# Window attention with one 64-column score tile a head, and value matmuls in quarters

## The chip, the cores and the metric

The kernel runs on one core of a Trainium2 chip. TensorE (PE) multiplies matrices out of SBUF into PSUM, VectorE (DVE) and ScalarE (ACT) work elementwise on SBUF and PSUM, GpSimd (POOL) on SBUF, and SyncE (SP) issues most transfers. The engines run side by side and wait for one another by semaphores; each executes its own instructions in the order in which they were written. The metric is the device time of one execution in microseconds.

## The reference

Two stages, one behind the other, all in fp32.

Attention with a sliding window: batch 8, heads 8, sequence 576, head width 64. A token attends to itself and the 63 tokens before it in its sequence.

```python
scores = scale * np.matmul(q, k.transpose(0, 1, 3, 2))
rel = pos[:, None] - pos[None, :]
mask = (rel >= 0) & (rel < window)          # window = 64
scores = np.where(mask, scores, -1000000000.0)
scores = scores - np.max(scores, axis=-1, keepdims=True)
attn = np.exp(scores)
attn = attn / (np.sum(attn, axis=-1, keepdims=True) + 1e-09)
return np.matmul(attn, v).astype(np.float32)
```

Then a mixture of experts on the 4608 rows of 512 columns: logits `x @ w_gate` plus a bias by modality, the best of 8 experts for each row, its softmax weight as a gate, and `gate * (relu(x @ w1[e]) @ w2[e])` with 1024 hidden columns.

## The kernel before, in words

The sequence is cut into blocks of 64 tokens, nine to a batch entry. Two neighbouring blocks make a pair, so that there are 36 pairs. A token of a block can attend to tokens of its own block that are not later than it, and to tokens of the block before that are less than 64 back. In its own block that is the lower triangle with the diagonal; in the block before it is the strict upper triangle. The first block of a batch entry has no block before it: those are blocks 0, 9, 18 and so on, and pairs 0, 4, 9, 13, 18, 22, 27 and 31 hold one.

The program is one loop over steps `s` (line 1023), written out by hand: no scheduler reorders it, and each engine's queue is the order of the text. Step `s` works on several pairs at once: scores of pair `s`, transposes of the probabilities of pair `s-1`, values and scaled rows of pair `s-2`, router logits of pair `s-3`, and routing (`route1` to `route3`) and scattering of rows to an expert-sorted scratch in DRAM behind that. Also in each step, q and k of a later group of four blocks are transposed (`heads_t`, `heads_out`), v of pair `s` is loaded (`load_v`), and from step 5 on pieces of two experts' weights are loaded and split in two parts (`weights`).

From step `FIRST = 12` on, expert work is put between the attention's pieces: `gap` takes the next piece of a generator (`slot_pieces`), four pieces a step. A piece is 12 matmuls of 256 columns (`first`, line 304) or 6 of 512 columns (`second`, line 326), each for a slot of 256 rows. After step 39 the rest of the expert work runs alone to the end.

What the change touches in a step:

- `scores` (line 596): for each of four pairs of heads, four matmuls in quarters of the array. The row half (64 partitions of q and k) is the head's parity `a`, the column half is the block `c` of the pair. Each multiplies 64 queries with 128 keys: a block's own 64 and the 64 of the block before. Parity `a` goes to PSUM bank `sp[a]`.
- `minima` (line 617): on VectorE, for each of eight heads, one instruction adds a mask of three variants, scales by -1/8, writes to SBUF and gives the row's minimum.
- `exps` (line 633): on ScalarE, eight exponentials with the row's minimum as bias; each also gives the row's sum. They are issued in three portions over the step.
- `probs_t` (line 642), called twice: four 128x128 transposes on TensorE into one bank (`turn`, line 470), and a copy to SBUF on ScalarE (line 647).
- `values` (line 660): 16 matmuls, one for each head and block, of 128 keys by 64 queries by 64 columns. The 128 keys of the pair's second block are the pair's own rows of v (`vo`); those of the first block need the block before, so that a second tile `ve` holds the upper half of the pair before (`swap_upper`, VectorE) and the lower half of this pair (`swap_v`, GpSimd). The result is a bank of its own, `ps_a`.
- `values_out` (line 673): VectorE scales the rows by the reciprocal of the sums into `xa`; `x_t` transposes these rows, `logits` multiplies them with the gate's weights.

PSUM has eight banks: two `tp`, two scores, one values, three `ps_m` (`em`, `y0`, `y1`) which before step 12 also serve transposes (`turn_bank`, line 514).

## Time and profile before

| | us |
|---|---|
| median of three runs | 622.34 (620.07 to 623.06) |
| the profiled execution | 621.29 |
| its span, first to last instruction | 619.6 |
| scores of step 1 begin | 14.54 |
| scores of step 11 begin | 68.15 |
| scores of the last pair begin | 318.22 |

The granted TensorE clock is 0.992 over the span. In the profile, an instruction's line is that of the program above; a row of the line of time has start, duration, engine, line, operation and tiles, and `x4` means four instructions merged. A fp32 matmul leaves two records, an fp32r matmul or a transpose one. TensorE's ends are modelled, its starts are not.

### The profile page before, as it was taken

The page shows a single profiled execution, that of the slowest core. Times are in us where ns is not written, and L with a number is a line of the kernel's source. Part 1 is how long each engine was busy: PE and PEld are TensorE (multiplying, and loading weights), DVE is VectorE, ACT ScalarE, POOL GpSimd, SP SyncE. Part 2 cuts the span into 40 slices and gives each one's busy share as a digit, 9 for nine tenths or more (in the row PEclk, how much of TensorE's full clock was granted, in tenths as well). Part 3 has the DMA queues.
Part 4 walks back from the last instruction along what each step waited for, and adds up shares of the span by engine and source line. Part 5 has one row for each costly group of instructions (what it writes and reads, how often), then busy time and mean ns, then how long its engine had stood idle before and what let it go on. Part 6 is the DMA issues. An engine that isn't in the chain of part 4 may idle for free. (4 is left out here: it accounts for less than half of the span.)

```text
span 619.6 us, 17314 instructions
## 1 busy us (share of the span) xinstructions
PE 603.5 (97%) x6365; PEld 542.2 (88%) x6365; DVE 381.8 (62%) x1486; ACT 297.4 (48%) x933; POOL 139.7 (23%) x315
## 2 busy tenths in 40 slices
PE   8999889999999999999999999999999999999996
PEld 5888778889898998989898899999999989999986
DVE  3899987877776877667656465323324734776622
ACT  3999886765757555636463111111112513554411
POOL 6333422042313320321223131011001101102202
PEclk7999999999999999999999999999999999999999
DMA  9999865764675754463313034522243534678300
GB/s 163 216 234 246 204 183 166 188 188 126 167 205 123 194 135 99 137 155 84 107 54 103 35 103 167 174 69 69 51 155 116 167 126 137 203 239 249 108 18 21
DMA packets 158983, 88.08 MB, mean 142 GB/s; under 512 B 122618, under 2 KB 141616, under 8 KB 158768
## 3 DMA queue, kind: packets, MB, share of 16 engines
q1 hardware_dynamic: 150272, 67.45, 43.1%
q0 software_dynamic: 5888, 18.93, 8.1%
q8 instruction: 51, 0.84, 0.6%
q10 hardware_dynamic: 2736, 0.58, 0.5%
q14 instruction: 36, 0.29, 0.2%
HBM read 67.49 MB, written 23.91 MB: 148 GB/s over the span
## 5 line engine op out<-in xcount | busy, mean ns | idle before, releaser
L326 PE MATMUL y<-Whi,hh 128*128 128x512 f32 x288 | 116.9, 406 | 0.0
L638 ACT ACTIVATE ss<-ss,mn 128x128 f32<-128x128 f32 x288 | 112.6, 398 | 4.0 <-DMA wg<-in_moe_w_gate_dram 3.3
L326 PE MATMUL y<-Wlo,hh 128*128 128x512 f32 x288 | 112.7, 391 | 0.0
L326 PE MATMUL y<-Whi,hl 128*128 128x512 f32 x288 | 112.5, 391 | 0.0
L337 POOL DMA_INDIRECT out_dram<-y,id x36 | 39.8, 1107 | 232.7 <-DVE y L334 159.9
L313 DVE SCALAR_TENSOR_TENSOR hl<-em,hh 128x512 fp32r<-128x512 f32 x50 | 34.5, 690 | 92.8 <-ACT hh L312 82.1
L304 PE MATMUL em<-xh,Whi 128*128 128x256 f32 x400 | 83.7, 290 | 0.0
L312 ACT ACTIVATE hh<-em 128x512 fp32r<-128x512 f32 x50 | 29.6, 592 | 105.2 <-PE em L304 86.9
L304 PE MATMUL em<-xl,Whi 128*128 128x256 f32 x400 | 79.3, 280 | 0.0
L304 PE MATMUL em<-xh,Wlo 128*128 128x256 f32 x400 | 79.1, 279 | 0.0
L647 ACT COPY pT<-tp 128x512 f32<-128x512 f32 x57 | 31.4, 589 | 70.2 <-PE tp L470 60.9
L626 DVE CUSTOM_DVE_ANT_0 ss<-sp,masks 128x128 f32<-128x128 f32 x288 | 63.5, 286 | 2.4 <-PE sp L612 2.3
L326 PEld LDWEIGHTS y<-Whi,hl 128*128 128x128 f32 x288 | 54.1, 188 | 12.2
L304 PEld LDWEIGHTS em<-xh,Whi 128*128 128x128 f32 x400 | 62.3, 189 | 1.8
L326 PEld LDWEIGHTS y<-Whi,hh 128*128 128x128 f32 x288 | 54.2, 188 | 8.2
L326 PEld LDWEIGHTS y<-Wlo,hh 128*128 128x128 f32 x288 | 54.2, 188 | 7.9
L304 PEld LDWEIGHTS em<-xl,Whi 128*128 128x128 f32 x400 | 60.9, 188 | 0.0
L304 PEld LDWEIGHTS em<-xh,Wlo 128*128 128x128 f32 x400 | 60.9, 188 | 0.0
L638 ACT ACTIVATION_READ_ACCUMULATOR ss<-ss,mn 128x1 f32 x288 | 56.0, 195 | 0.0
L773 POOL DMA_INDIRECT xs_scratch<-xa,idx x36 | 36.4, 1012 | 81.8 <-DVE lm L716 40.3
L312 ACT ACTIVATE hh<-sp 128x512 fp32r<-128x512 f32 x22 | 13.2, 598 | 75.9 <-PE sp L304 73.9
L668 PEld LDWEIGHTS av<-ve,pT 128*64 128x64 f32 x576 | 36.3, 138 | 13.2 <-issue 8.2
(240 smaller groups left out, 1211.3 us busy)
## 6 DMA issues: line engine op xcount, KB each, us to landing
xt<-xs_scratch SPq DMA_DIRECT2D x72, 128.0 KB
vo<-in_v_dram SPq DMA_DIRECT2D x32, 256.0 KB
y<-in_moe_w_dram SPq DMA_DIRECT2D x32, 256.0 KB
vo<-in_moe_w_dram SPq DMA_DIRECT2D x24, 256.0 KB
ss<-in_moe_w_dram SPq DMA_DIRECT2D x24, 256.0 KB
xs_scratch<-xs_scratch SPq DMA_DIRECT2D x8, 514.0 KB
pT<-in_moe_w_dram SPq DMA_DIRECT2D x16, 256.0 KB
qk<-in_k_dram SPq DMA_DIRECT2D x14, 256.0 KB
```

The lines of the kernel that those rows point to most:

```text
L304: nc.tensor.matmul(out=hb[:, i * TP:(i + 1) * TP], lhsT=w[buf][:, c0:c0 + P], rhs=x[:, c * TP:(c + 1) * TP], start=(n == 0), stop=(n == le ...
L312: nc.scalar.activation(out=hh, in_=hb, func=AF.Relu),
L313: nc.vector.scalar_tensor_tensor(out=hl, in0=hb, scalar=0.0, in1=hh.bitcast(F32), op0=ALU.max, op1=ALU.subtract)))
L326: nc.tensor.matmul(out=sl["y", t], lhsT=h[:, i * TP + t * P:i * TP + (t + 1) * P], rhs=w[buf][:, c0:c0 + DM], start=(k == 0 and n == 0), s ...
L337: ins = nc.gpsimd.indirect_dma_start(out=out, out_offset=bass.IndirectOffsetOnAxis(ap=sl["id"][:, t:t + 1], axis=0), in_=y, in_offset=None ...
L626: nc.vector.tensor_tensor_reduce(out=ss[a][:, hp, :], in0=sp[a][:, hp * P:(hp + 1) * P], in1=mask, scale=-1.0 / 8.0, scalar=3.0e38, op0=AL ...
L638: nc.scalar.activation(out=ss[a][:, hp, :], in_=ss[a][:, hp, :], func=AF.Exp, bias=mn[:, h:h + 1], scale=-1.0, accum_out=sm[:, h:h + 1])
L647: nc.scalar.copy(out=pT, in_=pp)
L668: nc.tensor.matmul(out=by_block(av)[c * W64:(c + 1) * W64, a, :, hp, :], lhsT=pT[:, i:i + W64], rhs=(vo if c else ve)[p][:, 2 * hp + a, :] ...
L773: ins = nc.gpsimd.indirect_dma_start(out=xs, out_offset=bass.IndirectOffsetOnAxis(ap=idx[:, j:j + 1], axis=0), in_=xg[j], in_offset=None)
```

## The change

Each score row needs 64 probabilities, not 128: where the own key `j` is allowed (not later than the query), key `j` of the block before is not, and the other way round. So both triangles fit in one 64-column tile a head.

- `scores` makes the same 16 matmuls, but writes the own columns and the other columns to two halves of each bank, over one two-bank tile `sp`.
- `minima` copies, by predicate, the other half's scores into the own half above the diagonal (`above`); at a batch edge it fills that block's rows with a large negative number instead, in two half-height copies. Then one maximum over 64 columns and one subtraction, which writes the heads side by side to SBUF.
- `exps` is one exponential of 128x512; the sums are a VectorE reduction (`exp_sums`).
- `probs_t` makes four transposes and one copy for all eight heads. GpSimd then makes two tiles: the part of the block before (`left_of`) and, in place, the part of the own block (`from_`).
- `values` makes, for each of four pairs of heads, four matmuls with the own part and four with the other part that add to them, all of 64 keys by 64 queries by 64 columns, in quarters of the array. A first block of a batch entry has no other part. The result goes into the other half of the score banks of the current step, which that step's `minima` has read.
- V is loaded as 64 keys of two head parities, in four transfers a pair, into four buffers instead of three; `ve` and both swaps are gone.
- `ps_a` is gone and `tp` has three banks; `ss` has two buffers and `pT` four, and the weights that are loaded late use `vo` and `pT`.
- Order: values come after the pair's minima, the transposes of probabilities and the exponential; logits and row transposes come later in the step; all copies of transposed heads go to ScalarE.

```diff
-        sp = [ps_s.tile([P, 512], F32, name=f"sp{a}") for a in range(2)]
+        sp = st[p, "sp"] = ps_s.tile([P, 2, 512], F32, name="sp")
...
-                    out=sp[a][c * W64:(c + 1) * W64, hp * P:(hp + 1) * P], lhsT=qT[rows, place(g + c, hp), :],
+                    out=halves_of(sp[c * W64:(c + 1) * W64, a])[:, :, hp, :], lhsT=qT[rows, place(g + c, hp), :],
...
+        for rows, data in lots:
+            n = rows.stop - rows.start
+            nc.vector.copy_predicated(
+                out=own[rows], mask=above[rows].bitcast(I32)[:, None, None, :].broadcast_to([n, 2, HP, W64]),
+                data=data[rows])
+        mx = small.tile([P, 2, HP], F32, name="mn")
+        nc.vector.reduce_max(out=mx, in_=own, axis=AX.X)
+        ss = work.tile([P, HP, P], F32, name="ss", bufs=2)
+        nc.vector.tensor_tensor(
+            out=heads_of(ss), in0=own, in1=mx[:, :, :, None].broadcast_to([P, 2, HP, W64]), op=ALU.subtract)
...
+    def exps(p):
+        ss = st[p, "s"]
+        nc.scalar.activation(out=ss, in_=ss, func=AF.Exp, scale=1.0 / 8.0)
...
+        for t, m in ((other, left_of), (own, from_)):
+            nc.gpsimd.tensor_tensor(
+                out=t.rearrange("p (x i) -> p x i", i=W64), in0=own.rearrange("p (x i) -> p x i", i=W64),
+                in1=m[:, None, :].broadcast_to([P, 2 * HP, W64]), op=ALU.mult)
...
+    def values(p, sp):
+
+        own, other = st.pop((p, "p"))
+        for hp in range(HP):
+            for o in range(2):
+                for r, c in ((0, 0), (1, 1), (0, 1), (1, 0)):
+                    g = 2 * p + c
+                    edge = g % BPB == 0
+                    if o and edge:
+                        continue
+                    rows = slice(r * W64, (r + 1) * W64)
+                    i = hp * P + c * W64
+                    g -= o
+                    nc.tensor.matmul(
+                        out=sp[c * W64:(c + 1) * W64, r, 256:512].rearrange(
+                            "p (a c d) -> p a c d", a=2, d=R32)[:, :, hp, :],
+                        lhsT=(other if o else own)[rows, i:i + W64],
+                        rhs=vo[g // 2][rows, g % 2, hp, :].rearrange("p (a d) -> p a d", a=2),
+                        start=(o == 0), stop=(o == 1 or edge))
...
         if s < NPR:
             scores(s)
+            sp = st[s, "sp"]
...
             minima(s)
...
+        if s < FIRST:
+            part(0)
         if s == FIRST:
             run_later()
         if n_gap > 0 and s != FIRST:
             gap(it, True)
+        if 1 <= s <= NPR:
+            sums(s - 1)
+            probs_t(s - 1, turn_bank(s))
+        if s < NPR:
+            exps(s)
         if 2 <= s < NPR + 2:
-            x_t(s - 2, turn_bank(s) if s != FIRST else ps_m.tile([P, 512], F32, name="y0"))
+            if sp is None:
+                sp = ps_s.tile([P, 2, 512], F32, name="sp")
+            values(s - 2, sp)
+            values_out(s - 2)
+        if s < NPR:
+            exp_sums(s)
         run_later()
         tick(2)
...
+        if s < FIRST:
+            part(1)
+            choice()
+        else:
+            part(0)
+            choice()
...
+        rows_t()
+        if s >= FIRST:
+            part(1)
```

More of the change, by code (lines that the diff above doesn't have):

```diff
@@ L617, in minima @@
     def minima(p):
-        sp = st.pop((p, "sp"))
-        mask = masks[:, 1 if 2 * p % BPB == 0 else 2 if (2 * p + 1) % BPB == 0 else 0]
-        ss = [work.tile([P, HP, P], F32, name="ss", bufs=3) for _ in range(2)]
-        mn = small.tile([P, H], F32, name="mn")
-        for u in range(H):
-            a, hp = divmod(u, HP)
-            h = 2 * hp + a
-            nc.vector.tensor_tensor_reduce(
-                out=ss[a][:, hp, :], in0=sp[a][:, hp * P:(hp + 1) * P], in1=mask,
-                scale=-1.0 / 8.0, scalar=3.0e38, op0=ALU.add, op1=ALU.min,
-                accum_out=mn[:, h:h + 1])
@@ L630, in minima @@
-        sm = small.tile([P, H], F32, name="sm")
-        st[p, "s"] = ss, mn, sm
-    def exps(p, us):
-        ss, mn, sm = st[p, "s"]
-        for u in us:
-            a, hp = divmod(u, HP)
-            h = 2 * hp + a
-            nc.scalar.activation(
-                out=ss[a][:, hp, :], in_=ss[a][:, hp, :], func=AF.Exp,
-                bias=mn[:, h:h + 1], scale=-1.0, accum_out=sm[:, h:h + 1])
-    def probs_t(p, a, pp):
-        ss = st[p, "s"][0][a]
+        sp = st[p, "sp"]
+        own, other = (sp[:, :, x * 256:(x + 1) * 256].rearrange("p a (h j) -> p a h j", j=W64) for x in range(2))
@@ new lines, in minima @@
+        edge = [c for c in range(2) if (2 * p + c) % BPB == 0]
+        lots = [(slice(0, P), other)]
+        if edge:
+            fills = negs[:, None, None, :].broadcast_to([P, 2, HP, W64])
+            lots = [(slice(c * W64, (c + 1) * W64), fills if c in edge else other) for c in range(2)]
+        for rows, data in lots:
[3 more added lines that the diff above has]
+                data=data[rows])
@@ L644, in probs_t @@
+    def probs_t(p, pp):
+        ss = st.pop((p, "s"))
         for hp in range(HP):
             turn(pp[:, hp * P:(hp + 1) * P], ss[:, hp, :])
-        pT = work.tile([P, HP * P], F32, name="pT", bufs=2)
-        nc.scalar.copy(out=pT, in_=pp)
-        st[p, "p", a] = pT
+        own = work.tile([P, HP * P], F32, name="pT", bufs=4)
+        nc.scalar.copy(out=own, in_=pp)
+        other = work.tile([P, HP * P], F32, name="pT", bufs=4)
+        for t, m in ((other, left_of), (own, from_)):
+            nc.gpsimd.tensor_tensor(
+                out=t.rearrange("p (x i) -> p x i", i=W64), in0=own.rearrange("p (x i) -> p x i", i=W64),
+                in1=m[:, None, :].broadcast_to([P, 2 * HP, W64]), op=ALU.mult)
+        st[p, "p"] = own, other
@@ L911, in tile_window_attn_moe @@
     nc.gpsimd.memset(by_group(kT)[:, 1, :, GBLK - 1, :], 0.0)
[L914 to L933 removed]
+    above, left_of, from_ = (const.tile([P, W64], F32, name=nm) for nm in ("above", "left_of", "from"))
+    for t, step, op in ((above, 1, ALU.is_gt), (left_of, -1, ALU.is_gt), (from_, 1, ALU.is_ge)):
+        nc.gpsimd.memset(t, 1.0)
+        for h in range(2):
+            rows = slice(h * W64, (h + 1) * W64)
+            nc.gpsimd.affine_select(
+                out=t[rows], in_=t[rows], compare_op=op, fill=0.0, base=0,
+                pattern=[[step, W64]], channel_multiplier=-step)
+    negs = const.tile([P, W64], F32, name="negs")
+    nc.gpsimd.memset(negs, NEG)
     nc.gpsimd.memset(first_oh, 0.0)
@@ L1031, in tile_window_attn_moe, with part, rows_t, choice @@
         R = (s - 5) // GB if s >= 5 and j == 1 else -1
-        if 1 <= s < FIRST:
-            swap_upper(s - 1)
-        if 2 <= s < NPR + 2:
-            values(s - 2)
-            if s <= FIRST:
-                values_out(s - 2)
-        if 3 <= s < NPR + 3:
-            logits(s - 3, turn_bank(s) if s != FIRST else ps_m.tile([P, 512], F32, name="y0"))
-            if (s - 3) % GB == GB - 1:
-                route1((s - 3) // GB)
-        if FIRST < s < NPR + 2:
-            values_out(s - 2)
+        def part(i):
+            if not heads:
+                return
+            tp = turn_bank(s)
+            heads_t(G, *heads[i], tp)
+            heads_out(tp, G, *heads[i], nc.scalar.copy)
+        def rows_t():
+            if 2 <= s < NPR + 2:
+                x_t(s - 2, turn_bank(s))
+        def choice():
+            if 3 <= s < NPR + 3:
+                logits(s - 3, turn_bank(s))
+                if (s - 3) % GB == GB - 1:
+                    route1((s - 3) // GB)
+        sp = None
         if s < NPR:
             scores(s)
+            sp = st[s, "sp"]
             if s == FIRST:
```

137 lines of the change are left out of this document (39 added, 98 removed).

## The prediction

> **What bounds the kernel now.** I read the page's first part, then the stretches of the span, then TensorE's line of time.
>
> ```profile
> PE 603.5 (97%) x6365; PEld 542.2 (88%) x6365; DVE 381.8 (62%) x1486; ACT 297.4 (48%) x933; POOL 139.7 (23%) x315
> ...
> core 0: us, PE busy (x) PEld busy (x) DVE busy (x) ACT busy (x) POOL busy (x), PEclk, DMA share, GB/s
> 14.54:68.15 53.61, 50.50 (x992) 45.28 (x991) 49.80 (x281) 50.78 (x204) 19.78 (x38) 0.99 0.99 231
> 345.00:600.00 255.00, 255.00 (x1656) 232.20 (x1656) 124.20 (x257) 73.62 (x134) 35.47 (x76) 1.00 0.43 132
> ```
>
> There are two regimes. Before the expert work begins (step 12) TensorE, VectorE, ScalarE and the DMA engines are all over 90% busy together: no one of them is the bound, and a step is a tightly packed loop. The stretch 14.54 to 68.15 is ten steps, from the scores of step 1 to those of step 11: 5.36 us a step, with 4.98 us of VectorE, 5.08 of ScalarE and 1.98 of GpSimd in each. From step 12 on TensorE alone is full; after the attention (345 to 600) it is busy all of 255 us on work that the diff leaves alone. So whatever the attention's end moves by, the kernel's end moves by, and I sum that.
>
> ```profile
> 68.15 1.10 PE L612 MATMUL sp<-kT,qT 64*64 64x128 f32 x32
> ...
> 253.74 0.39 PE L326 MATMUL y<-Wlo,hh 128*128 128x512 f32 x1
> 253.96 0.40 PE L326 MATMUL y<-Whi,hl 128*128 128x512 f32 x1
> 254.28 0.27 PE L668 MATMUL av<-ve,pT 128*64 128x64 f32 x1
> 254.29 0.27 PE L668 MATMUL av<-vo,pT 128*64 128x64 f32 x1
> ...
> 255.22 0.22 PE L668 MATMUL av<-vo,pT 128*64 128x64 f32 x1
> 255.27 0.59 PE L697 MATMUL tp<-wg,xaT 128*64 128x8 f32 x16
> 255.79 1.10 PE L612 MATMUL sp<-kT,qT 64*64 64x128 f32 x32
> 256.82 1.09 PE L470 MATMUL tp<-ident_r,ss 128*128 128x128 f32 x8
> 257.67 0.48 PE L304 MATMUL em<-xh,Whi 128*128 128x256 f32 x2
> 258.00 0.40 PE L304 MATMUL em<-xh,Wlo 128*128 128x256 f32 x2
> 258.23 0.40 PE L304 MATMUL em<-xl,Whi 128*128 128x256 f32 x2
> ...
> 259.18 0.60 PE L470 MATMUL tp<-ident_r,xa 128*128 128x128 f32 x4
> 259.53 0.48 PE L304 MATMUL em<-xh,Whi 128*128 128x256 f32 x2
> ...
> 266.45 1.10 PE L612 MATMUL sp<-kT,qT 64*64 64x128 f32 x32
> ```
>
> This is one steady step, 255.79 to 266.45 (10.66 us). Starts matter, since ends are modelled: values hold TensorE 0.99 us (254.28 to 255.27), logits 0.52, scores 1.03, eight transposes 0.85, a piece of expert work 1.51 (257.67 to 259.18), four transposes 0.35.
>
> **The change, part by part, in a steady step.**
>
> *Transposes.* Eight become four: 0.85 - 0.35 = 0.50 us less on TensorE, which sets the end.
>
> *Values.* 32 records (16 matmuls, two records each) of 128 rows become 64 records of 64 rows, 48 in a pair with a batch edge. Scores already run in the same four quarters, with the same row half to one bank: their 32 records start within 1.10 - 0.27 = 0.83 us, 27 ns apart. The old values need 0.99 us for 16 turns of two records. If four quarters run at once, 64 records are again 16 turns: 0.99 us, no change. If instead each record costs the 27 ns of a score, 64 take 1.7 us, 0.75 more. I take 0: a score moves 128 columns, a value 64, so the score's row is no floor for it; 0.75 is kept for the range.
>
> *More changes of array shape.* Values, logits and scores now stand in one run; after the change each stands alone between pieces of 128-row work.
>
> ```profile
> 342.66 0.39 PE L326 MATMUL y<-Wlo,hh 128*128 128x512 f32 x1
> 342.89 0.39 PE L326 MATMUL y<-Whi,hl 128*128 128x512 f32 x1
> 343.21 0.64 PE L697 MATMUL tp<-wg,xaT 128*64 128x8 f32 x16
> 343.78 0.51 PE L304 MATMUL em<-xh,Whi 128*128 128x256 f32 x2
> 344.12 0.40 PE L304 MATMUL em<-xh,Wlo 128*128 128x256 f32 x2
> ```
>
> Logits alone, late in the kernel: the expert matmul ahead holds 0.32 us instead of 0.23 (342.66 to 342.89), and the first behind it 0.34 instead of the 0.23 of 258.00 to 258.23. So a border costs about 0.1. There are three borders now (into values, logits to scores, scores to transposes) and six afterwards: +0.30 us. The bounds are 0.15 and 0.45.
>
> *The wait of values.* This decides. Values are written into the "other" half of the two score banks, while VectorE still works through the "own" half of the same banks: predicated copy, maximum, subtraction. Does the matmul wait for the first only, or for all three? The start of the trace shows how two engines share a bank: VectorE and ScalarE each copy their own half of the columns.
>
> ```profile
> 7.90 0.42 DVE L593 COPY kT<-tp 128x256 f32<-128x256 f32 x1 [6.68 <-PE tp L470]
> 8.24 0.42 DVE L593 COPY qT<-tp 128x256 f32<-128x256 f32 x1
> ...
> 8.36 0.39 ACT L593 COPY kT<-tp 128x256 f32<-128x256 f32 x1 [3.26 <-DVE kT L593]
> 8.69 0.39 ACT L593 COPY qT<-tp 128x256 f32<-128x256 f32 x1
> ```
>
> ScalarE starts 0.04 us after VectorE's copy ends, twice, though the columns are disjoint: the order is kept by bank. I take it to hold for a matmul's write as well, so values wait for the subtraction. By the Trainium skill, PSUM — Partial Sum Buffer, "PSUM bank collisions raise a hardware error", PSUM is to be guarded by bank and partition quadrant and not by address; these rows agree, no run here shows a matmul's write yet, and without that rule the sum would be the rival "by columns" below.
>
> ```profile
> L626 DVE CUSTOM_DVE_ANT_0 ss<-sp,masks 128x128 f32<-128x128 f32 x288 | 63.5, 286 | 2.4 <-PE sp L612 2.3
> L679 DVE TENSOR_TENSOR xa<-av,rw 128x512 f32<-128x512 f32 x36 | 24.9, 691 | 2.6 <-PE av L668 0.5 <-DMA xs_scratch<-xa,idx 0.3
> L542 DVE COPY ve<-vo 64x512 f32<-64x512 f32 x35 | 15.3, 438 | 1.1
> L577 DVE COPY qT<-tp 128x512 f32<-128x512 f32 x27 | 18.5, 687 | 17.9 <-PE tp L470 17.7
> L638 ACT ACTIVATE ss<-ss,mn 128x128 f32<-128x128 f32 x288 | 112.6, 398 | 4.0 <-DMA wg<-in_moe_w_gate_dram 3.3
> L647 ACT COPY pT<-tp 128x512 f32<-128x512 f32 x57 | 31.4, 589 | 70.2 <-PE tp L470 60.9 <-PE sp L612 8.2 <-PE em L470 0.8
> ...
> 63.95 0.69 DVE L679 TENSOR_TENSOR xa<-av,rw 128x512 f32<-128x512 f32 x1
> ...
> 64.70 0.66 PE L470 MATMUL y<-ident_r,xa 128*128 128x128 f32 x4 [0.59 <-DVE xa L679]
> ```
>
> A VectorE pass over 128x512 from PSUM takes 0.69 us (L679, L577). The trace has no predicated copy and no wide reduction; I bound each between 0.44 (L542, the quickest of that width) and 1.38 (two passes), and take 0.69, the row of that shape from PSUM. From the first score: results 1.10, hand-over 0.04, three passes with 0.04 between them 2.15, hand-over to TensorE 0.06 (xa ends at 64.64, its transpose starts at 64.70): values may start at 3.35. TensorE gets there after scores 1.03, one piece 1.51, four transposes 0.35 and a border 0.09: 2.98. So it stands 0.37 us in each step; every expert piece behind it on that queue waits too. In a pair with a batch edge the predicated copy is two half-height ones, so 0.73 more. The bounds are no wait and 2.5 us.
>
> *Hidden here.* ScalarE loses the narrow exponentials (112.6 / 36 = 3.13 us a pair) and one copy of transposed probabilities, and gains one wide exponential and one and a half head copies; at 0.59 each (L647) that is 3.13 + 0.59 - 0.59 - 0.88 = 2.25 us less a pair. Logits and the transposes of the scaled rows move behind values; routing hangs on them, and the expert rows that it places are fetched steps later. Were that cover gone, step 12 would start late once, by at most the half step of the move, 2.7 us. GpSimd gets two masks of 128x512 and loses the swap:
>
> ```profile
> L988 POOL TENSOR_TENSOR bias_sel<-bias_sel,y 128x288 f32<-128x288 f32 x1 | 0.8, 798 | 0.1
> L528 SPq DMA_DIRECT2D vo<-in_v_dram x32: 175/389/1317, 10.5 to 312.2; - x32
> L532 SPq DMA_DIRECT2D vo<-in_v_dram x8: 616/630/699, 26.5 to 270.7; - x8
> ```
>
> Worked out from L988, 512 elements take 1.4 us, 2.8 a pair, read only one step later; uncovered they would cost that much a step. V comes in four issues a pair instead of one or two, each 0.39 to 0.63 us on SP: up to 2.1 us more, hidden in 10.66.
>
> Steady sum: -0.50 + 0 + 0.30 + 0.37 = +0.17 us over 24 steps (12 to 35) = 4.1; five of their pairs (13, 18, 22, 27, 31) have an edge, 5 x 0.73 = 3.7. Together **+7.8**.
>
> **Steps 1 to 11.** Here the same chain becomes a loop: scores cannot overwrite the banks before VectorE has scaled the values that lie in them, and the transpose of the scaled rows stands ahead of the next scores. Scores 1.10 + 0.04, three passes 2.15 + 0.06, values 1.16 (254.28 to 255.22 and its 0.22) + 0.04, scaling 0.69 + 0.06, transposes 0.35, border 0.10: **5.75 us** against 5.36 measured. VectorE's own load falls from 4.98: minima 63.5 / 36 = 1.76 less, half swap 0.43 less, one and a half head copies 1.03 less, four passes 2.76 more, edges 0.14 more: 4.66. It fits beside the loop, but VectorE stands idle about 1 us in it while values run, so there is little slack either. ScalarE's relief gains nothing, since the loop does not pass through it at length. 11 x 0.39 = 4.3, and pairs 4 and 9 with an edge 2 x 0.73 = 1.5: **+5.8**. The bounds are -7 (a step falls to VectorE's 4.66) and +12 (a half us more a step).
>
> Sum: 7.8 + 5.8 = +13.6 us. The profiled execution took 621.29 (span 619.6 and 1.7 around it), which gives 634.9; the median of the runs is 622.34, 1.05 higher, so I forecast **636.0**, by itself between 628 and 645.
>
> **The rivals.**
>
> *By columns (faster).* The matmul waits only for the predicated copy, the last reader of the columns that it overwrites. Then values may start at 1.10 + 0.04 + 0.69 + 0.06 = 1.89, before TensorE arrives at 2.98: no wait, no edge cost. Steady: 24 x -0.20 = -4.8. Early: values leave the loop, which falls to 5.75 - 1.16 = about 4.6, and VectorE's 4.66 binds; at the 93% that it reaches now that is 5.0 a step, 11 x -0.36 = -4.0. Time 622.3 - 8.8 = 613.5. For it: the work was laid out with only part of the bank in use; against it: the L593 rows.
>
> *One record at a time.* Quarter matmuls of 64 columns start no closer than the 27 ns of a score's record: 0.75 more for each full pair, 0.3 at an edge. Of the 26 pairs valued from step 12 on, 21 are full: 15.8 + 1.5 = 17.3, on top of the wait: 653. It decides from about 15 ns a record (16 turns of 59 ns over 64) upward. Against it: neighbouring records of the two column halves start 0.01 us apart now. The Trainium skill, TensorE: Matmul & The Clock Gate, "Wait — 56ns, not 53.3ns?", states that start-to-start never drops below about 25 ns; by an estimate from it values would take 1.6 us. Sustained runs here (scores 27, values 31 ns a record) agree, but do not show a floor.
>
> *SP paces the early stage.* DMA share is 0.99 there. If 2.1 us of added issue in each of 11 steps is not covered and a third shows, that is 8 us more: 644.
>
> **Chances.** Forecast 0.55, by columns 0.25, one record at a time 0.12, SP 0.08. The range 612 to 647 holds the forecast's own range, most of the faster case and SP's, and leaves out the slowest. Within 0.5% (3.1 us) counts as no change, about what a measurement can tell. Faster: most of "by columns" and a trace of the forecast, 0.25; within 0.5%: 0.10; slower: 0.65.
>
> **What would show it.** In the steady steps: the first value matmul with idle time before it, released by VectorE's subtraction, about 0.4 us, and 1.1 at an edge; none of it, or released by the predicated copy, and the forecast falls. The 64 value records spanning about 1.0 us, or 1.7 by the second rival. Expert matmuls of 0.32 ahead of each of three islands. Steps before 12 of 5.7 to 6.0 us with the order scores, three VectorE passes, values, scaling; ScalarE at 5.08 - 2.25 = 2.8 us a step there. The stretch after the attention as long as now.

## The result, and the profile after

The changed kernel takes 669.09 us (667.48 to 670.07) against 622.19 us (620.07 to 623.06) for the kernel before on the same chip: a ratio of 1.075, 95% interval 1.0707 to 1.0794. The forecast was 636.0, in a range of 612 to 647. The direction was right, and the loss is more than three times as large as forecast. The profiled execution took 670.07, with a span of 668.3. A fourth timed execution took 1180.37 us at a full granted clock; range and ratio leave it out, the median of all four counts it (without it, it is 668.11), and its cause is not known.

The first and second part of the page of the changed kernel, engines' busy time and the granted clock in 40 slices:

```profile
PE 615.9 (92%) x7245; PEld 539.7 (81%) x7245; DVE 379.1 (57%) x976; ACT 220.4 (33%) x408; POOL 208.4 (31%) x347
...
PEclk9689879989999999999999999999999999999998
```

TensorE has 12 us more of busy time in a span that is 49 us longer, so that most of the loss is TensorE standing still, and in the first ten slices (of 16.7 us each) its clock is below full again and again. VectorE lost 2.7 us, ScalarE 77 us, and GpSimd gained 69 us: none of the three became the bound.

The stretches between starts of scores, before and then after: steps 1 to 11, step 12, steps 13 to 16, steps 17 to 34. The columns are those of the prediction's second view.

```profile
14.54:75.51 60.97, 55.92 (x1096) 49.98 (x1095) 56.87 (x319) 57.46 (x230) 20.91 (x40) 0.99 0.94 222
75.51:85.34 9.83, 7.97 (x127) 7.41 (x124) 9.33 (x35) 7.89 (x28) 4.68 (x9) 1.00 0.61 174
85.34:129.08 43.74, 42.65 (x555) 38.02 (x552) 33.93 (x145) 30.25 (x99) 8.96 (x19) 1.00 0.65 175
129.08:318.22 189.14, 189.14 (x2477) 170.56 (x2474) 133.46 (x630) 111.43 (x398) 50.22 (x101) 1.00 0.54 142
```

```profile
13.51:94.03 80.52, 59.56 (x1274) 49.50 (x1274) 57.03 (x165) 35.28 (x65) 40.51 (x51) 0.88 0.72 174
94.03:105.92 11.89, 10.62 (x153) 9.32 (x152) 11.29 (x21) 6.46 (x13) 6.32 (x9) 0.68 0.47 133
105.92:157.24 51.32, 45.58 (x649) 39.38 (x648) 31.85 (x84) 20.38 (x40) 18.36 (x24) 0.93 0.57 153
157.24:363.57 206.33, 192.43 (x2916) 165.95 (x2915) 130.15 (x377) 73.14 (x137) 84.79 (x116) 1.00 0.49 127
```

The loss of 48.7 us of span is therefore: 1.0 gained before step 1, then +19.6, +2.1, +7.6 and +17.2 in the four stretches, and +3.4 behind the last scores (668.3 - 363.57 against 619.6 - 318.22). In the first stretch the clock is 0.88 where it was 0.99, and the DMA engines fell from 0.94 to 0.72: they are no longer full. In the last one TensorE stands 206.33 - 192.43 = 13.9 us where it stood not at all.

Two late steps of the changed kernel on TensorE, the first with a batch edge, and VectorE in these and in the step behind them, which has scores at 295.99:

```profile
273.07 1.10 PE L595 MATMUL sp<-kT,qT 64*64 64x128 f32 x32
...
277.23 1.16 PE L671 MATMUL sp<-vo,pT 64*64 64x64 f32 x64 [1.01 <-issue]
278.32 0.50 PE L304 MATMUL em<-xh,Whi 128*128 128x256 f32 x2
...
284.85 1.10 PE L595 MATMUL sp<-kT,qT 64*64 64x128 f32 x32
...
288.41 1.16 PE L671 MATMUL sp<-vo,pT 64*64 64x64 f32 x64 [0.41 <-issue]
```

```profile
276.44 0.69 DVE L624 TENSOR_TENSOR ss<-sp,mn 128x512 f32<-128x512 f32 x1
...
284.84 1.29 DVE L196 TENSOR_TENSOR xl<-xt,xh 128x512 fp32r<-128x512 f32 x2 [0.59 <-ACT xh L195]
286.16 0.70 DVE L618 COPY_PREDICATED sp<-above,sp 128x512 f32<-128x512 int32 x1
...
287.62 0.69 DVE L624 TENSOR_TENSOR ss<-sp,mn 128x512 f32<-128x512 f32 x1
...
297.27 0.75 DVE L334 TENSOR_SCALAR y<-y,gate 128x512 f32<-128x512 f32 x1
297.94 0.69 DVE L618 COPY_PREDICATED sp<-above,sp 128x512 f32<-128x512 int32 x1
```

Values start 0.10 us after the subtraction ends, in both steps (276.44 + 0.69 = 277.13 and 277.23; 288.31 and 288.41), although the subtraction reads other columns than values write. It is so in every step from 3 to 34, within 0.01 us. The profile names other releasers, or none ("issue"); the times show that it is the subtraction. So the columns do not decide, as forecast. Whether the order is kept by bank or by tile no run tells, since `sp` is one tile over both banks. The last two rows show what can come on top: the scaling of expert rows stands ahead of the predicated copy on VectorE, which starts 1.95 us behind the first score instead of 1.17. The 64 records of values hold TensorE 277.23 to 278.32, 1.09 us.

An early step, on TensorE and then on VectorE:

```profile
50.92 1.10 PE L595 MATMUL sp<-kT,qT 64*64 64x128 f32 x32
...
54.34 1.16 PE L671 MATMUL sp<-vo,pT 64*64 64x64 f32 x48 [1.29 <-POOL xa L778]
55.43 0.66 PE L470 MATMUL tp<-ident_r,Whi 128*128 128x128 f32 x4
56.02 0.64 PE L703 MATMUL em<-wg,xaT 128*64 128x8 f32 x16
56.59 0.66 PE L470 MATMUL y<-ident_r,xa 128*128 128x128 f32 x4
57.17 0.45 PE L595 MATMUL sp<-kT,qT 64*64 64x128 f32 x8
```

```profile
52.09 0.70 DVE L618 COPY_PREDICATED sp<-above,sp 128x512 f32<-128x512 int32 x1 [0.77 <-PE sp L595]
...
53.55 0.69 DVE L624 TENSOR_TENSOR ss<-sp,mn 128x512 f32<-128x512 f32 x1
...
55.54 0.69 DVE L685 TENSOR_TENSOR xa<-sp,rw 128x512 f32<-128x512 f32 x1 [1.14 <-PE sp L671]
```

This is the loop that was forecast, scores, three passes, values, scaling, transposes, and it takes 6.25 us (50.92 to 57.17) rather than 5.75. The scaled rows are ready at 56.23, 0.06 of hand-over later they could be read, but TensorE reaches their transposes only at 56.59, because transposes of heads and the logits (55.43 to 56.59) stand ahead of them in its queue; and these transposes, a border before the scores, hold it 0.58 us and not 0.45.

### The profile page after: what moved, and what is told of

It is laid out like the page before. It is cut to its first block, busy times and chain, and to the rows that moved or that the text cites. A ratio compares the mean times of both kernels' runs of the same rounds, so it can differ in the third digit from the quotient of the medians.

```text
span 668.3 us, 18024 instructions
## 1 busy us (share of the span) xinstructions
PE 615.9 (92%) x7245; PEld 539.7 (81%) x7245; DVE 379.1 (57%) x976; ACT 220.4 (33%) x408; POOL 208.4 (31%) x347
## 4 chain that ended last, share of the span: by engine, by line
PE 81%; DVE 5%; issue 5%; ACT 3%; POOL 3%; DMA 2%; POOLq 0%; ACTq 0%; DVEq 0%
PE y L326 28%; PE em L304 21%; PE sp L304 9%; PE sp L671 7%; PE tp L470 7%; PE sp L595 3%; PE tp L703 2%; DMA Whi<-in_k_dram 1%; PE y L377 1%; POOL xs_scratch L779 1%; ACT xaT L695 1%; POOL out_dram L337 1%; DVE hl L313 1%; DMA y<-in_moe_w_dram 1%; ACT hh L312 1%
## 5 line engine op out<-in xcount | busy, mean ns | idle before, releaser
L647 POOL TENSOR_TENSOR pT<-pT,left_of 128x512 f32<-128x512 f32 x36 | 45.9, 1275 | 148.3 <-ACT pT L644 147.7
L304 PE MATMUL em<-xh,Whi 128*128 128x256 f32 x400 | 85.2, 295 | 1.1 <-DVE hl L313 1.1
L671 PE MATMUL sp<-vo,pT 64*64 64x64 f32 x2176 | 45.9, 235 | 36.5 <-issue 19.4
L671 PEld LDWEIGHTS sp<-vo,pT 64*64 64x64 f32 x2176 | 41.7, 146 | 44.2 <-issue 22.9
L685 DVE TENSOR_TENSOR xa<-sp,rw 128x512 f32<-128x512 f32 x36 | 24.9, 692 | 43.8 <-PE sp L671 43.7
L779 POOL DMA_INDIRECT xs_scratch<-xa,idx x36 | 36.2, 1006 | 40.4 <-DVE y L334 12.9
L595 PE MATMUL sp<-kT,qT 64*64 64x128 f32 x1152 | 41.9, 284 | 7.1 <-DVE ss L624 5.1
L647 POOL TENSOR_TENSOR pT<-pT,from 128x512 f32<-128x512 f32 x36 | 46.5, 1291 | 2.8
```

Source lines behind the costliest of these rows:

```text
L304: nc.tensor.matmul(out=hb[:, i * TP:(i + 1) * TP], lhsT=w[buf][:, c0:c0 + P], rhs=x[:, c * TP:(c + 1) * TP], start=(n == 0), stop=(n == le ...
L595: nc.tensor.matmul(out=halves_of(sp[c * W64:(c + 1) * W64, a])[:, :, hp, :], lhsT=qT[rows, place(g + c, hp), :], rhs=kT[rows, win(c, hp), ...
L647: nc.gpsimd.tensor_tensor(out=t.rearrange("p (x i) -> p x i", i=W64), in0=own.rearrange("p (x i) -> p x i", i=W64), in1=m[:, None, :].broa ...
L671: nc.tensor.matmul(out=sp[c * W64:(c + 1) * W64, r, 256:512].rearrange("p (a c d) -> p a c d", a=2, d=R32)[:, :, hp, :], lhsT=(other if o ...
L685: nc.vector.tensor_tensor(out=xa[:, 0:DM].rearrange("p (g x d) -> p g x d", g=2, d=R32), in0=st.pop((p, "av"))[:, :, 256:512].rearrange("p ...
L779: ins = nc.gpsimd.indirect_dma_start(out=xs, out_offset=bass.IndirectOffsetOnAxis(ap=idx[:, j:j + 1], axis=0), in_=xg[j], in_offset=None)
```

## The experiments

Starts of scores give the stretches of every run, from its profiled execution; the time is the median of the timed runs. The first recorded expectations count steps 1 to 11 as ten steps, up to the scores of step 11: by that count the changed kernel has 71.8 us, own banks 62.3, six more matmuls 67.9. The table counts eleven.

| kernel | time | steps 1-11 | step 12 | 13-16 | 17-34 |
|---|---|---|---|---|---|
| before | 622.2 | 60.97 | 9.83 | 43.74 | 189.14 |
| after | 669.1 | 80.52 | 11.89 | 51.32 | 206.33 |
| own banks early | 671.7 | 68.59 | 23.27 | 51.51 | 207.98 |
| values behind second piece | 653.1 | 80.42 | 15.78 | 51.23 | 190.54 |
| six more matmuls | 673.1 | 75.43 | 16.21 | 50.87 | 208.41 |
| no edge mask | 669.7 | 72.75 | 18.01 | 50.70 | 206.08 |
| before, v in four of 64 rows | 639.9 | 70.14 | 17.73 | 43.79 | 190.37 |
| before, v in four of 128 rows | 633.4 | 62.57 | 13.90 | 44.35 | 191.79 |
| half of v from ScalarE | 672.1 | 77.81 | 13.57 | 50.86 | 206.55 |
| own banks, v from ScalarE | 664.5 | 71.84 | 13.48 | 49.21 | 206.46 |
| three edits | 647.7 | 67.74 | 20.41 | 47.59 | 191.61 |
| chain | 651.9 | 82.98 | 14.31 | 46.50 | 187.09 |
| hybrid | 645.2 | 74.06 | 14.76 | 44.33 | 189.10 |
| v in one | 667.9 | 74.64 | 15.42 | 51.26 | 207.05 |
| v in one, two edits | 634.3 | 65.85 | 11.15 | 47.16 | 190.61 |
| v in one, hybrid | 634.0 | 69.29 | 12.07 | 45.15 | 186.27 |
| v in one, six more matmuls | 660.6 | 72.40 | 10.49 | 49.11 | 206.66 |

**Own banks for the early values.**

```diff
+            if s < FIRST:
+                sp = [ps_m.tile([P, 512], F32, name=f"y{r}")[:, 0:256] for r in range(2)]
             values(s - 2, sp)
```

Two of the banks that transposes took in turn go to the values for it.

> Steps 2 to 11 write values into two banks of their own (those of the expert sums, free before step 12) instead of the other half of the score banks; the rows are scaled in two operations of 128x256. Theory 'loop by bank': the loop scores, three VectorE passes, values, scaling is broken, since values no longer wait for the subtraction and scores no longer wait for the scaling. Steps fall to VectorE's own work, about 5.1 us instead of 6.5, so scores 1 to 11 take about 55 instead of 71.7 us, TensorE's stands of 1.5 to 3 us and the half clock there go, and the time is about 652 us. Rival 'SP and the DMA engines pace the early stage': the same 71 us, 669. Rival 'the clock of its own accord': idle shrinks but the granted clock stays near 0.88 and the stretch over 65 us, 663 or more.

Measured: 671.7 us. The loop went, steps 1 to 11 fell by 12 us to 68.59, and step 12 took all of it back. TensorE's longest wait there, and VectorE's and SP's line of time around it:

```profile
PE sp L671 <- issue: 11.3, 1, 11.3
```

```profile
91.64 1.31 DVE L266 STREAM_TRANSPOSE xt<-xt 128x512 f32<-128x512 f32 x2 [7.95 <-DMA xt<-xs_scratch]
...
94.30 0.69 DVE L624 TENSOR_TENSOR ss<-sp,mn 128x512 f32<-128x512 f32 x1
```

```profile
80.53 2.58 SPq L526 DMA_DIRECT2D vo<-in_v_dram  x4
84.15 2.83 SPq L211 DMA_DIRECT2D xt<-xs_scratch  x5
```

The first expert's rows (`xt`) are fetched by SP behind v's four transfers, 8.3 us after step 11 began (75.85); before, it was 2.4 us (70.59 against 68.15). They are there 7.5 us after the fetch began to be issued, of which SP's issuing takes 2.8; what holds the rest was not looked into. VectorE's transposition of these rows waits 7.95 us for them, the minima of step 12 stand behind it on VectorE, and values wait for the minima. So behind the first limit lies a second one, which later runs (v's transfers by themselves, v in one transfer) put down to SP's queue. Neither theory had both.

**Values behind the second expert piece.**

```diff
-        if 2 <= s < NPR + 2:
+        if 2 <= s <= FIRST:
             rows_of_values()
...
             if s != FIRST:
                 gap(it, True)
+        if FIRST < s < NPR + 2:
+            rows_of_values()
```

> From step 13 on the values and the scaling of their rows stand behind the second expert piece, not the first; before that nothing changes. Theory 'values wait by bank, and VectorE's queue ahead of the predicated copy makes the wait longer than forecast': the wait, 0.84 us a step on the mean, is covered by 1.5 us more of TensorE's work, and steps 17 to 35 take about 10.7 us instead of 11.46; with 23 steps about 17 us less, 652 us. Rival 'the loss is borders and the order of work': the wait moves to whatever stands behind (the second piece's own operands or the transposes of scaled rows), and under 5 us is won, 664 or more.

Measured: 653.1 us, ratio to the kernel before 1.0492 (1.0348 to 1.0636). Late steps of the changed kernel waited as in the first two rows, those of this one as in the third:

```profile
PE sp L671 <- issue: 7.8, 13, 1.0
PE sp L671 <- POOL rs L655: 6.1, 5, 1.6
```

```profile
PE sp L671 <- issue: 0.2, 1, 0.2
```

Steps 17 to 34 take 190.54 us, 10.59 each, against 206.33. The bank wait is 15.8 us there, 0.88 a step. The rest of the late loss is 190.54 - 189.14 = 1.4 us, which holds the borders and the saved transposes together.

**Six more matmuls in the early stands, and no mask at batch edges.**

```diff
+        if 2 <= s < FIRST:
+            warm_bank = turn_bank(s)
+            for _ in range(6):
+                nc.tensor.matmul(out=warm_bank, lhsT=idle[:, 0:P], rhs=idle[:, 0:512], start=True, stop=True)
```

```diff
-        edge = [c for c in range(2) if (2 * p + c) % BPB == 0]
+        edge = []
```

> In each of steps 2 to 11 TensorE gets six more bf16 matmuls of 128x512 (about 1.3 us, no part of the result) where it stands still and waits for VectorE's subtraction. Theory 'the half clock is what made the early loop longer than the forecast 5.75': with no stand over 1 us the granted clock stays at 1.0 through steps 1 to 11, and the stretch falls from 71.7 to about 63 to 65 us; 661 us. Rival 'TensorE at half clock only fills the idle, the loop is VectorE's': the stretch stays at 70 to 73 us and the time within 2 us of 669, or above it.

> Leaves out the mask on the block ahead of a batch's first block: every pair has one predicated copy over all 128 rows, also the seven pairs with a batch edge after the first (4, 9, 13, 18, 22, 27, 31) and pair 0; the weights of those rows come out otherwise. It prices the second predicated copy. By the forecast 0.73 us for each edge: 7 x 0.73 = 5 us less, 664. Theory 'an edge also sets off a half clock, since TensorE stands 0.7 us longer at it': the steps of pairs 4 and 9 fall from 8 to 9 us to about 6.5, the late edges by about 1 us, and the half clock near 30, 75 and 92 us goes: 10 to 15 us less, 655 to 659. Rival 'edges cost nothing on the path': 669.

Measured: 673.1 and 669.7 us, no gain: the times are the rivals', though the stretch of the first is 67.9 us, between its theory and its rival. Both shortened steps 1 to 11, by 5 and 8 us, and both lost it in step 12 (16.21 and 18.01 us), as own banks did; step 13 starts at 105.3 to 105.9 us in these and in the changed kernel alike. So neither run alone prices its cause. The late edges can be read all the same: steps 18, 22, 27 and 31 take 10.96 to 11.06 us without the second copy and 11.69 to 11.78 with it, 0.71 to 0.73 each. The early edges cost more, as the theory of the second run said: without the mask steps 4 and 9 fell from 8.46 and 9.05 us to 6.25 and 6.99. In the changed kernel the granted clock is half in parts of both (from 40.3 and from 74.4 us, 3.4 us each); where it stays full in step 4, with v in one transfer (below), that step takes 6.98 us against 6.25 for the step before it, 0.73 more.

**V's transfers by themselves.** The kernel before, with four transfers of 64 rows and half the heads:

```diff
-            nc.sync.dma_start(out=t, in_=v_v[g0 // BPB, s0:s0 + P])
+            for r in range(2):
+                hs = slice(r * HP, (r + 1) * HP)
+                nc.sync.dma_start(
+                    out=t[i * W64:(i + 1) * W64, hs], in_=v_v[g // BPB, s0:s0 + W64, hs])
```

> The kernel before, with v loaded in four transfers of 64 rows and half the heads, as after the change, instead of one or two; nothing else differs. It prices the added issues on SP by themselves. Theory 'SP': where the first experiment freed the loop, SP issued without a gap and steps went no lower than 6.3 to 6.7 us; the same issues here lengthen steps 5 to 11 from 5.4 to about 6.3 and bring the first expert's rows and weights later, 8 to 14 us more, 630 to 636. Rival 'the issues hide', as the sum of the prediction had it: within 3 us of 622.

Measured: 639.9 us, ratio 1.0282 (1.025 to 1.0313), 17.5 us with no other edit. One early step of SP's queue in this run, from v to v, and the stretches of steps 1 to 11 and of step 12:

```profile
62.41 3.37 SPq L530 DMA_DIRECT2D vo<-in_v_dram  x4
65.83 2.25 SPq L562 DMA_DIRECT2D Whi<-in_k_dram  x4
68.33 0.37 SPq L107 DMA_DIRECT2D y<-in_moe_w_dram  x1
68.86 3.46 SPq L530 DMA_DIRECT2D vo<-in_v_dram  x4
```

```profile
15.32:85.46 70.14, 62.06 (x1095) 56.03 (x1095) 56.98 (x316) 58.75 (x234) 20.27 (x40) 0.90 0.76 184
85.46:103.19 17.73, 10.26 (x127) 9.69 (x125) 10.44 (x36) 9.26 (x30) 4.60 (x9) 0.71 0.67 171
```

SP issues from 62.41 to 68.70 with 0.3 us of gaps: 6.45 us from v to v, more than the 5.4 us of a step before. What it issues comes late: 9.2 us by step 12, then 7.9 us more in step 12, where the first expert's rows are behind it and VectorE waits 5.53 us for them. From step 13 on 1.3 us are added. The second run on this has four transfers too, of 128 rows and two heads each:

```diff
+            for r in range(4):
+                hs = slice(2 * r, 2 * r + 2)
+                nc.sync.dma_start(out=t[:, hs], in_=v_v[g0 // BPB, s0:s0 + P, hs])
```

> The kernel before with v of each pair in four transfers of 128 rows and two heads (two of 64 rows at a batch edge, as before): as many issues as after the change, of another shape. Theory 'the number of transfers counts, each waits for its place among those in flight and for SP': 635 to 641 us, as with four transfers of 64 rows (639.9). Rival 'a transfer of 64 rows is slow to issue, 0.63 against 0.39 us': SP's share grows by 1.2 us a step only, 624 to 629.

Measured: 633.4 us, ratio 1.0201 (1.0155 to 1.0247), 11.7 us, between the two theories. Four of them take SP 1.73 to 2.17 us in steps 6 to 11, four of 64 rows 2.58 to 3.46. Number and shape both count; the loss goes with SP's time, but SP's time and the number in flight were not told apart.

**Part of v from ScalarE's queue.** First two of the four in the changed kernel; then all four, with own banks for the early values.

```diff
-                nc.sync.dma_start(
+                (nc.scalar if r else nc.sync).dma_start(
```

> The changed kernel with two of the four transfers of v of each pair issued from ScalarE's queue, which has slack, instead of SP's. Theory 'loop and SP bind the early steps at the same height (6.25 us)': steps 1 to 11 hardly fall, below 2 us together, since the loop stays, but the weights reach ScalarE sooner in step 16, whose 17.2 us fall to about 13 to 15: 662 to 667 us. Rival 'SP alone sets the early steps': 1.2 us off each of ten steps, 655 or less. Rival 'SP does not matter': 669.

> The first experiment (values before step 12 in banks of their own) with all four transfers of v of a pair issued from ScalarE instead of SP, in order on one queue. Theory 'the loop and SP's issues are two limits of one height in steps 5 to 12, and taking one away shows the other': with both gone early steps take 5.4 to 5.7 us, scores of step 12 start at 76 to 80 us and of step 13 at 88 to 93 instead of 105.4; the late steps keep the bank wait: 652 to 658 us. Rival 'the first expert's rows or its weights come at 92 us of themselves': step 13 again at 104 to 106 us, 668 to 672.

Measured: 672.1 us, no gain, and 664.5 us, 7 less than with own banks alone, where 14 to 20 were expected. In the second run ScalarE issues the four transfers, and then goes on:

```profile
60.72 3.22 ACTq L526 DMA_DIRECT2D vo<-in_v_dram  x4
63.98 0.61 ACT L562 COPY kT<-tp 128x512 f32<-128x512 f32 x1 [2.85 <-DMA vo<-in_v_dram]
```

The issues now take ScalarE's time, 3.22 us here (60.72 to 63.94), and its copy starts 0.04 us behind the last of them. The profile puts four such waits in steps 1 to 12, 10.8 us, down to v's transfers themselves; each ends 0.04 us after the last issue, so that it is the issuing that the copies stand behind. By the Trainium skill, DMA: Bandwidth & Descriptors, "Issuing engines are not separate DMA queues", another issuing engine saves only the issuing time, since all share the same 16 DMA engines. These two runs are in line with that, at most 7 us, but do not show the sharing; that this time is "usually small" beside the transfer does not fit here: it is 0.6 of 2.9 us from issue to landing, and the early steps ran into it.

**Versions that were to win the loss back.** Three edits together (own banks early, values behind the second piece late, half of v from ScalarE); a chain of logits, values and scores at the start of each step, with values in banks of their own; and the early order of the first with the late order of the second.

```diff
+        if s >= FIRST:
+            choice()
+            rows_of_values()
         if s < NPR:
             scores(s)
...
-        rows_t()
-        if s >= FIRST:
+        if s < FIRST:
+            rows_t()
+        else:
             part(1)
```

> Three edits together: values before step 12 in banks of their own, values after it behind the second expert piece, half of v issued from ScalarE. Theory 'loop and SP bind the early steps together, the bank wait costs the late ones': early steps about 5.5 us, so that scores of step 12 start near 78 us rather than 94; the first expert's rows follow, and the gain of the first experiment is no longer lost in step 12; late steps 10.6 us; 630 to 638 us. Rival 'the first expert's rows come at their own time': step 13 starts at 105 us whatever came before, and the time is 650 to 654.

> A version meant to beat both: one merged score layout, four transposes and masks as changed, but logits, values and scores in one run at the start of a step as in the kernel before, values in banks of their own throughout, half of v issued from ScalarE. By the terms measured so far: no bank wait and no early loop, half as many borders, 0.5 us of transposes saved: late steps about 10.1 to 10.3 us against 10.51 before (7 to 10 us less), early steps 5.4 as before: 612 to 620 us. Rival 'SP, ScalarE's issues and the masks hold the early steps at 6.3': 625 to 632.

> Steps before 12 as in the run beside it (order of the changed kernel, values in banks of their own, v issued from ScalarE), steps from 12 on with logits, values and scores in one run at the start and values in two free transpose banks. Theory: late steps 10.05 to 10.2 us as in the version before it (10.51 in the kernel before, 0.35 to 0.45 us less in each of 23), early steps 5.4 to 5.7: 613 to 622 us. Rival 'step 13 comes at 105 us whatever the early steps do': 636 to 640.

Measured: 647.7, 651.9 (ratio 1.0472, 1.0434 to 1.051) and 645.2 us (1.0372, 1.0334 to 1.041). All three lie above their theories' ranges, and none in its rival's (650 to 654, 625 to 632, 636 to 640). Step 13 starts at 104.3, 113.5 and 104.2 us, in the first and third about where the rivals had it (105), and no version reached the kernel before. The chain's late steps are the first below the kernel before:

```profile
160.00:347.09 187.09, 184.50 (x2926) 164.21 (x2921) 129.89 (x394) 72.50 (x136) 85.42 (x116) 1.00 0.55 142
```

That is 10.39 us a step against 10.51, and 9.96 to 10.3 in 10 of the 18 steps. Its early steps, with half of v on ScalarE, are the longest of all, 82.98 us.

**V in one transfer.** The changed kernel, then with own banks and the second piece, then the hybrid, each with v loaded as before. The values are then of other heads and blocks.

```diff
-            for r in range(2):
-                nc.sync.dma_start(
-                    out=t[r * W64:(r + 1) * W64, c], in_=v_v[b, r, g * W64:(g + 1) * W64])
+        if g + 1 < BPB:
+            nc.sync.dma_start(out=x, in_=v_v[b, g * W64:(g + 2) * W64])
```

> The changed kernel with v loaded as in the kernel before, one transfer of 128 rows (two at a batch edge). It leaves out the new placing of v by head halves: the rows that the values read then hold other heads and blocks, and only the time is meant. Theory 'v's transfers and the bank wait are two separate losses': the 17.5 us that the four transfers cost in the kernel before come off here too, steps 5 to 11 fall to the loop's own 5.75 to 6.25, step 13 starts near 92 us instead of 105.9, the late steps stay at 11.46: 648 to 655 us. Rival 'the loop holds the early steps anyway': under 5 us are won, 664 or more.

> The same loading of v (again values of other heads and blocks), and the two edits of the first two experiments: values before step 12 in banks of their own, values after it behind the second expert piece. Theory: with transfers, loop and bank wait all gone only the borders are left, late steps 10.58 us (10.51 before), early steps 5.2 to 5.5: 619 to 627 us, about the kernel before. Rival 'a further cost in steps 12 to 17 (the first expert's rows, masks on GpSimd)': 632 or more.

> The last hybrid (late steps with logits, values and scores in one run, values in free transpose banks; early values in banks of their own) with v loaded as in the kernel before, values again of other heads and blocks. It prices what four transposes instead of eight are worth when nothing else is paid. Theory: late steps 10.1 to 10.25 us, early steps 5.2 to 5.5, 612 to 618 us, below the kernel before. Rival: the masks and the wide passes cost elsewhere, 622 or more.

Measured: 667.9 us, ratio 1.0725 (1.0683 to 1.0767); 634.3 (1.0204, 1.0171 to 1.0237); 634.0 (1.0213, 1.0178 to 1.0248). All three are the rivals. The first run's steps 1 to 11 and 12, and the second's four stretches:

```profile
13.37:88.01 74.64, 56.72 (x1274) 47.27 (x1275) 55.16 (x165) 34.36 (x63) 40.58 (x51) 0.94 0.80 191
88.01:103.43 15.42, 13.29 (x154) 11.98 (x153) 10.83 (x21) 7.01 (x13) 6.32 (x9) 0.53 0.38 114
```

```profile
14.25:80.10 65.85, 58.23 (x1275) 47.84 (x1274) 55.32 (x167) 34.33 (x64) 40.00 (x50) 0.94 0.85 206
80.10:91.25 11.15, 7.83 (x154) 7.07 (x153) 10.85 (x30) 5.91 (x12) 7.34 (x11) 1.00 0.53 150
91.25:138.41 47.16, 43.21 (x648) 37.04 (x647) 31.34 (x85) 20.82 (x41) 19.26 (x23) 1.00 0.63 161
138.41:329.02 190.61, 190.39 (x2915) 165.09 (x2915) 137.04 (x377) 73.32 (x137) 85.04 (x117) 1.00 0.55 140
```

Here is why single edits won nothing. Step 13 starts at 105.9 us with shared banks and four transfers, at 105.4 with own banks alone, at 103.4 with one transfer alone, and at 91.2 with both, 85.3 in the kernel before (the other edit of that run begins with step 13). The two limits lie side by side, and the slower sets the time. But with one transfer the first expert's rows were in time (VectorE's transposition of them did not wait), and step 12 took 15.42 us at a clock of 0.53. That was the next question:

```diff
+        if 2 <= s <= FIRST:
+            warm_bank = turn_bank(s)
+            for _ in range(6):
+                nc.tensor.matmul(out=warm_bank, lhsT=idle[:, 0:P], rhs=idle[:, 0:512], start=True, stop=True)
```

> The changed kernel with v loaded in one transfer as in the kernel before (values of other heads and blocks, as said there), and six more bf16 matmuls of 128x512 in each of steps 2 to 12, where TensorE waits for the subtraction. With v in one transfer alone the first expert's rows come in time, yet step 12 took 15.4 us, TensorE at half clock from 85 to 102 us. Theory 'the half clock that TensorE's stands bring along is paid in step 12, the first one that TensorE fills': kept warm, steps 1 to 11 take 68 to 71 us instead of 74.6, step 12 10.5 to 12 us, and step 13 starts at 92 to 96 us instead of 103.4: 656 to 661 us against 668. Rival 'step 12 is long because of its own operands': step 13 stays past 101 us, 665 or more.

Its steps 1 to 11 and step 12:

```profile
13.33:85.73 72.40, 66.80 (x1325) 50.98 (x1335) 54.44 (x160) 34.59 (x64) 40.67 (x51) 0.98 0.80 194
85.73:96.22 10.49, 9.07 (x158) 7.62 (x158) 10.20 (x26) 5.91 (x12) 6.63 (x9) 1.00 0.41 126
```

Measured: 660.6 us (1.0611, 1.0583 to 1.0639), 7.4 less than without the added matmuls. Time and step 12 are the theory's; step 13 at 96.2 and steps 1 to 11 at 72.4 lie a little above its ranges. More work on TensorE made the kernel faster, with the clock up: step 13 starts 7.2 us earlier, 2.2 of it from steps 1 to 11 and 4.9 from step 12. Steps 5 to 8 kept their length (6.32 to 6.52 us, against 6.32 to 6.48), and there the clock is full in both runs, so that the loop's length is not the clock's; steps 9 and 11 fell from 8.93 and 8.67 to 7.65 and 7.53.

## Why the prediction was right or wrong

**The wait of values: the mechanism was right, the size was not.** Values do wait for the subtraction, though it reads other columns; its passes take 0.69 us each, so that the banks are free 3.3 us behind the first score where the first of them starts in time (1.17 + 2.15); "by columns" is refuted. Where VectorE starts on time TensorE stands 0.26 to 0.27 us in a step without an edge (0.37 forecast), and an edge costs 0.72 (0.73 forecast); the 0.41 of the second step above holds 0.14 of VectorE being late, so that its nearness to 0.37 is chance. For steps 17 to 34 the forecast's own terms give 18 x 0.37 + 4 x 0.73 = 9.6 us; the second experiment took 15.8. The term that failed is "three passes" counted from the first score: in 9 of these 18 steps VectorE comes 0.14 to 1.4 us late to the predicated copy, 6.2 us in all, behind `xl` or the scaling of expert rows (284.84 and 297.27 above), and TensorE waits for that too. The sum put this at nothing.

**Borders: mis-sized.** The late steps without a wait are 10.59 us against 10.51. With 0.50 us of transposes saved, borders and what goes with them cost about 0.58 rather than 0.30; no run took a border away by itself. The forecast's working for the border behind an island does not hold: it set a first expert matmul (0.34) against a second one (0.23), and the first one behind the eight transposes in the step that it shows, where no shape changes, holds TensorE 0.33 as well (257.67 to 258.00). Together with the first point the steady step was forecast at +0.17 without edges, and measured at +0.96 with them.

**Values in quarters: right.** 64 records hold TensorE 1.09 us, border included, 17 ns each, where 32 held it 0.99. "One record at a time" had them at 27 ns and 1.7 us and is refuted; nor do these quarters keep to the 25 ns from start to start that the prediction quotes from the Trainium skill, TensorE: Matmul & The Clock Gate, "Wait — 56ns, not 53.3ns?".

**The early loop: the order was right, the sum was short.** 5.75 forecast, 6.25 in the step above: 0.30 us for logits and transposes of heads ahead of the rows' transposes (56.29 to 56.59), 0.13 for the transposes and their border (0.58 instead of 0.45), and 0.07 because values start 3.42 us behind the scores rather than 3.35. The largest is a piece of TensorE's queue that the sum left out. Six of the eleven steps take 6.25 to 6.56 us. The other five (1, 2, 4, 9 and 11) take 42.5 together, where the forecast's terms give 30.2 with both edges, and they hold most of the shortfall. In step 11 VectorE is still splitting a weight (`Wlo`) when the scores are there:

```profile
87.24 0.68 DVE L119 TENSOR_TENSOR Wlo<-y,Whi 128x512 fp32r<-128x512 f32 x1
87.84 0.69 DVE L618 COPY_PREDICATED sp<-above,sp 128x512 f32<-128x512 int32 x1
90.08 1.16 PE L671 MATMUL sp<-vo,pT 64*64 64x64 f32 x48 [2.67 <-POOL pT L647]
```

The predicated copy starts 2.56 us behind the first score (85.28) instead of 1.17, in step 9 1.85, in steps 1 and 2 5.56 and 2.28. That is the same step that failed in the late stage, VectorE's start, and in parts of all five the granted clock is half on top.

**"SP paces the early stage": the rival with a chance of 0.08 had one of the missing causes.** The step that failed is "V comes in four issues ..., up to 2.1 us more, hidden in 10.66". That cover is right for late steps alone. In steps 5 to 11 SP's queue is longer than a step, and what stands last in it, the fetch of the first expert's rows, is due in step 12. V's four transfers alone cost the kernel before 17.5 us; the rival priced them at 8 for the changed one. In the changed kernel they lie beside the loop and are not added to it: taking them away alone won 1.2 us, an amount that can't be told from none.

**The half clock: not in the prediction at all.** The wait was priced at the time of standing. But the stands make TensorE's clock fall, and step 12, the first that TensorE fills, is then done in part at half speed (clock 0.68 over it; 0.53 with v in one transfer). Keeping it up won 7.4 us in the last experiment, 4.9 of it in step 12.

**What is left over.** With v in one transfer and both waits gone the loss is still 12.5 us, in the profiled executions' spans 12.9: 4.9 in steps 1 to 11, 1.3 in step 12, 3.4 in steps 13 to 16, 1.5 in the late steps, 2.1 behind the last scores, less 0.3 at the start. In the changed kernel 5.9 us of the 7.6 in steps 13 to 16 are step 16 (17.22 us against 11.37). There ScalarE waits 3.0 us for a weight's transfer, the cast of the rows stands behind it, VectorE's `xl` waits for that, and the minima and values behind `xl`; and the granted clock is half for 6.8 us from 146.1, when values start at 147.11 after a stand of 3.97 us. This was read in the trace, and no run took it away; step 16 took 13.9 to 18.9 us in all runs with the changed layout. Of the 3.4 us behind the last scores most is work that moved there and waits: in the new order the values of three pairs stand behind them and not of two (192 records of half the rows against 64, 1.2 us more of TensorE), the logits of one pair more (0.7), and TensorE waits 0.9. A load of v in fewer transfers with the new placing was not tried on the chip.

## What to carry to other kernels

Price a change of a transfer's shape on the queue that issues it, step by step, with all that stands behind it, and ask what is due last there; a step with slack on the average may have none in the stage where it counts. When a loop and a queue are near the same length, taking either away may win nothing, as here: test them together before you call either harmless. A wait on a matrix engine that was always busy can cost more than its length: here the clock came down with the waits, and the next full stretch paid. And count a wait from when the engine that ends it can start, with what stands ahead in its own queue.

## What the hardware did that was not expected

The longest stand of TensorE in steps 5 to 11 of the changed kernel was 2.7 us (step 9 and step 11, before values), and the granted clock fell to half at 74.4 us for 3.4 us and at 91.5 us for 10.2 us:

```profile
74.40:77.80 3.40, 3.00 (x70) 2.58 (x70) 1.42 (x4) 0.63 (x1) 1.22 (x2) 0.50 0.79 172
91.50:101.70 10.20, 8.93 (x138) 7.10 (x138) 9.35 (x20) 4.38 (x8) 5.69 (x9) 0.50 0.72 183
```

By the Trainium skill, TensorE: Matmul & The Clock Gate, "Part 1: The HAM clock gate", the clock falls after an idle window of about 3.4 us. Here shorter stands in a loop with more idle time around them sufficed; the trace agrees with that page's other remark, in "A second HAM failure mode: psum-queue depth-cycling", that frequent short idles do it as well.

A transfer of v of 64 rows and 64 KB takes SP longer to issue than one of 128 rows with four times the bytes: 0.615 us in the median after the change, 0.389 in the kernel before.
